# Attention and a two-layer MoE block on one core: the first two chunks interleaved, weights decoded by pairs of steps, and the first batch's GpSimd work moved to VectorE

## The chip, the cores and the metric

The kernel runs on one core of a Trainium2 chip. The time is the device time of one execution, in microseconds; the median over the runs is compared. The core has five engines: TensorE (PE, matmuls), VectorE (DVE), ScalarE (ACT), GpSimd (POOL), and SyncE (SP), which here issues every DMA.

## The reference, cut to what matters

```python
# q, k, v: (8 batches, 8 heads, 576 positions, 64)
q_d = q.reshape(B, H, 144, 4, D).mean(axis=3)          # k_d, v_d likewise
out_d = sm_attn(q_d, k_d, v_d)                         # softmax attention on 144 positions
out_up = np.repeat(out_d, 4, axis=2)
scores = np.where(abs(pos[:, None] - pos[None, :]) < 4, scale * q @ k.T, -1e9)
out_local = softmax(scores) @ v                        # seven keys per position
x = (out_up + out_local).transpose(0, 2, 1, 3).reshape(4608, 512)
h = x @ w_in                                           # 512 x 2048
g = np.maximum(h, 0.0) + alpha * np.minimum(h, 0.0)    # alpha: one number per hidden column
out = g @ w_out                                        # 2048 x 512
```

All inputs are fp32. Both MoE products are made from a high and a low part of each operand: high by high, high by low, low by high, so three matmuls each.

## The kernel before, in words

**Tokens and chunks.** The 4608 tokens are worked on in 18 chunks of 256. A chunk has 8 steps, one for each pair of 128-column blocks of the hidden layer. `h_step` makes 24 matmuls of 128x256 (line L642) into one PSUM tile. After it, ACT multiplies by the slope (L651), DVE takes the maximum (L654, the "relu" below: a tile `t` and two instructions for each step), ACT rounds to the high part `gh` (L656) and POOL subtracts to get the low part `gl` (L97, called through `sub`). `out_step` makes 12 matmuls of 128x512 (L690) into two PSUM tiles that add up over the chunk's 8 steps; after the eighth, ACT copies them to `sg` (L695) and SP stores them (L698). h runs AH = 2 steps ahead of out. The steps are numbered through, so `t8` is the relu of the first step of the second chunk and `t16` that of the third.

**Where x comes from.** The first 576 tokens (batch 0) are made by `first_batch`, four pairs of heads hp 0 to 3, on tiles that lie over the whole batch; this gives x for the first two chunks and a rest of 64 tokens for the third (`place_rest`). All other tokens come in units of 192 tokens, u = 3 to 23, from `local`: products of q and k on DVE (L551, with sums L553), a softmax whose small tiles lie in PSUM bank "l" (`lb`, L566 to L575), products of p and v (L593, L596, L598), a last sum into `x` (L600), then transposes on PE (`xp`), the sum with the downsampled part (`xf`, L615), and high and low parts `xh` (ACT) and `xl` (POOL, L97). A copy of q lies in PSUM bank "q" (`qp`). Chunk 2 needs units 3 and 4, and the downsampled attention of batch 1.

**Downsampled attention.** For batches 1 to 7 and each pair of heads, `load_sums` brings q, k and v in six loads (L228) through a ring of three `ld` buffers. POOL adds four positions into one (L100); what follows uses PE, ACT and a few small DVE instructions (`dnb` L279, `drs` L285).

**Weights.** w_in and w_out come as fp64 words, and are decoded in 32 pieces of 128x512: ACT makes an absolute value (L152), DVE runs four instructions (L153 to L156), ACT makes the high part, and DVE or POOL the low part (L204 for w_out, L210 for w_in on DVE, L97 on POOL). The raw words go through three slots. Pieces come in quarters n = 0 to 3 of the hidden columns, each quarter serving two steps: first four pieces of w_in, then four of w_out.

**First batch's engines.** Tables of letters give POOL (p) or DVE (v) for each pair of heads: sums of q and k of hp 2 and 3 (`FQ`, L408 and L410), sums of v of all pairs (`FV`, L426 and L430), the multiply by the reciprocal (`FMUL`, L454) and the low parts of x (`FLO`, L485) on POOL. `POOL_LO` gives some of the w_in low parts to POOL.

**Order.** Each engine runs its instructions in one fixed order. A scheduler lays that order out when the program is built, from its own model of times and from priorities (`high_priority` offsets such as PP, DP and HP). On the chip an instruction that waits holds up everything behind it on its engine. SP issues the loads and stores one after the other in the same way.

## Time and profile before

| | us |
|---|---|
| median of three runs (1134.49, 1140.88, 1140.39) | 1140.39 |
| profiled execution, its time | 1138.52 |
| profiled execution, span of the trace | 1136.7 |
| PE busy | 1005.7 |
| DVE busy | 861.4 |
| POOL busy | 526.4 |
| ACT busy | 454.7 |
| first relu of chunk 0 starts | 111.9 |
| copy of chunk 0's sums starts | 199.5 |
| copy of chunk 1's sums starts | 248.1 |
| first relu of chunk 2 starts | 251.0 |
| first relu of chunk 3 starts | 320.4 |

A time in the lower rows is counted from the start of the span. The trace's rows name an engine, a line of the kernel, the operation, and the tiles as output<-inputs. In rows of a timeline the first number is the start and the second the duration, and a bracket gives how long the engine had been idle and which instruction or transfer let it go on.

### The profile page before, as it was taken

The page shows a single profiled execution, that of the slowest core. Times are in us where ns is not written, and L with a number is a line of the kernel's source. Part 1 is how long each engine was busy: PE and PEld are TensorE (multiplying, and loading weights), DVE is VectorE, ACT ScalarE, POOL GpSimd, SP SyncE. Part 2 cuts the span into 40 slices and gives each one's busy share as a digit, 9 for nine tenths or more (in the row PEclk, how much of TensorE's full clock was granted, in tenths as well). Part 3 has the DMA queues.
Part 4 walks back from the last instruction along what each step waited for, and adds up shares of the span by engine and source line. Part 5 has one row for each costly group of instructions (what it writes and reads, how often), then busy time and mean ns, then how long its engine had stood idle before and what let it go on. Part 6 is the DMA issues. An engine that isn't in the chain of part 4 may idle for free.

```text
span 1136.7 us, 17891 instructions
## 1 busy us (share of the span) xinstructions
PE 1005.7 (88%) x6402; PEld 879.8 (77%) x6402; DVE 861.4 (76%) x1467; ACT 454.7 (40%) x1223; POOL 526.4 (46%) x633
## 2 busy tenths in 40 slices
PE   5857797898768999889999999989999989999995
PEld 5646675696657898777888888878888878899994
DVE  7999496597847889678878988779887778895110
ACT  5767344242323443333444334344343425333221
POOL 4787474333434644544555543555537244333221
PEclk9756889798968999899999999999999989999998
DMA  8944612222222222221223222323222212100000
GB/s 181 240 150 145 189 43 86 65 83 76 66 92 77 87 100 87 92 87 65 80 95 109 85 80 89 105 76 101 88 92 82 96 58 78 54 19 19 1 20 19
DMA packets 57503, 98.26 MB, mean 86 GB/s; under 512 B 19910, under 2 KB 25286, under 8 KB 57414
## 3 DMA queue, kind: packets, MB, share of 16 engines
q1 hardware_dynamic: 57414, 97.12, 27.1%
q8 instruction: 50, 0.82, 0.3%
q14 instruction: 39, 0.32, 0.1%
HBM read 87.67 MB, written 9.44 MB: 85 GB/s over the span
## 4 chain that ended last, share of the span: by engine, by line
PE 53%; DMA 20%; DVE 11%; POOL 6%; SPq 4%; issue 3%; ACT 2%; ACTq 0%; POOLq 0%; DVEq 0%
PE o L690 26%; PE h L642 22%; DMA ldk<-in_k 10%; DMA q<-in_q 4%; DMA ldq<-in_q 3%; POOL gl L97 2%; SPq L348 2%; DVE temp L155 1%; SPq L499 1%; POOL ldv L100 1%; DVE temp L153 1%; PE pv L266 1%; DVE temp L156 1%; PE xp L607 1%; DMA raw<-in_moe_w_out 1%
## 5 line engine op out<-in xcount | busy, mean ns | idle before, releaser
L97 POOL TENSOR_TENSOR gl<-t,gh 128x512 fp32r<-128x512 f32 x144 | 187.0, 1301 | 238.5 <-ACT gh L656 221.3
L654 DVE SCALAR_TENSOR_TENSOR t<-h,sign,t 128x256 f32<-128x256 f32 x288 | 125.6, 478 | 165.1 <-ACT t L651 159.3
L690 PE MATMUL o<-woh,gl 128*128 128x512 f32 x576 | 193.7, 414 | 45.1 <-POOL gl L97 45.0
L651 ACT ACTIVATE t<-h,slope 128x256 f32<-128x256 f32 x288 | 120.3, 469 | 244.4 <-PE h L642 159.4
L642 PE MATMUL h<-xh,wih 128*128 128x256 f32 x1152 | 201.1, 291 | 1.0 <-DVE t L654 0.7
L690 PE MATMUL o<-woh,gh 128*128 128x512 f32 x576 | 190.2, 407 | 10.3 <-ACT gh L656 10.3
L642 PE MATMUL h<-xh,wil 128*128 128x256 f32 x1152 | 194.3, 288 | 1.0 <-DVE wil L210 1.0
L690 PE MATMUL o<-wol,gh 128*128 128x512 f32 x576 | 191.2, 409 | 0.0
L642 PE MATMUL h<-xl,wih 128*128 128x256 f32 x1152 | 188.0, 285 | 0.0
L642 PEld LDWEIGHTS h<-xh,wih 128*128 128x128 f32 x1152 | 174.0, 196 | 14.4 <-DVE t L654 2.4
L690 PEld LDWEIGHTS o<-woh,gl 128*128 128x128 f32 x576 | 110.4, 195 | 75.8 <-POOL gl L97 51.7
L642 PEld LDWEIGHTS h<-xh,wil 128*128 128x128 f32 x1152 | 163.1, 194 | 1.9 <-DVE wil L210 1.2
L642 PEld LDWEIGHTS h<-xl,wih 128*128 128x128 f32 x1152 | 159.9, 192 | 0.3
L656 ACT CAST gh<-t 128x512 fp32r<-128x512 f32 x144 | 89.4, 621 | 148.5 <-PE o L690 78.6
L551 DVE TENSOR_TENSOR qk<-k,qp 128x768 f32<-128x768 f32 (+1 forms) x126 | 135.0, 1081 | 0.0
L553 DVE TENSOR_REDUCE ls<-qk 128x12 f32<-128x768 f32 (+1 forms) x126 | 133.5, 1080 | 0.2
L690 PEld LDWEIGHTS o<-wol,gh 128*128 128x128 f32 x576 | 111.1, 195 | 24.9 <-issue 0.2
L690 PEld LDWEIGHTS o<-woh,gh 128*128 128x128 f32 x576 | 102.3, 194 | 25.2 <-ACT gh L656 10.5
L598 DVE TENSOR_TENSOR lb<-lb,pv 128x384 f32<-128x384 f32 x210 | 117.9, 562 | 4.0
L100 POOL TENSOR_TENSOR ldk<-ldk 72x256 f32<-72x256 f32 x56 | 45.2, 808 | 153.7 <-DMA ldk<-in_k 143.3
L596 DVE TENSOR_TENSOR pv<-v,lb 128x1152 f32<-128x1152 f32 x84 | 96.8, 1152 | 2.5
L100 POOL TENSOR_TENSOR ldq<-ldq 72x256 f32<-72x256 f32 x56 | 42.8, 774 | 80.6 <-DMA ldq<-in_q 80.4
(146 smaller groups left out, 1194.3 us busy)
## 6 DMA issues: line engine op xcount, KB each, us to landing
k<-in_k SPq DMA_DIRECT2D x41, 384.0 KB
v<-in_v SPq DMA_DIRECT2D x41, 384.0 KB
raw<-in_moe_w_in SPq DMA_DIRECT2D x16, 512.0 KB
raw<-in_moe_w_out SPq DMA_DIRECT2D x16, 512.0 KB
ldq<-in_q SPq DMA_DIRECT2D x56, 144.0 KB
ldk<-in_k SPq DMA_DIRECT2D x56, 144.0 KB
ldv<-in_v SPq DMA_DIRECT2D x56, 144.0 KB
q<-in_q SPq DMA_DIRECT2D x42, 192.0 KB
```

The costliest lines, as they stand in the source:

```text
L97: nc.gpsimd.tensor_tensor(o, a, b, op=ALU.subtract)
L100: nc.gpsimd.tensor_tensor(o, a, b, op=ALU.add)
L348: nc.sync.dma_start(qk[hp][:, i, :, e, :], bass.AP(src.tensor, (2 * hp + e) * HEAD, [[512, 72], [64, 8], [1, 64]]))
L551: nc.vector.tensor_tensor(pr[:, :nd], window(kt, half, d0, nd), qp.unsqueeze(1).to_broadcast([128, nd, 2, 192]), op=ALU.mult)
L553: nc.vector.tensor_reduce(out=s[:, half, d0:d0 + nd, :].rearrange("p a b -> p (a b)"), in_=pr[:, :nd].rearrange("p a h (t d) -> p (a h t) ...
L596: nc.vector.tensor_tensor(pr[:, :nd], window4(vt, half, d0, nd), prob(half, d0, nd), op=ALU.mult)
L598: nc.vector.tensor_tensor(acc, acc, pr[:, i], op=ALU.add)
L642: nc.tensor.matmul(ph[:, j], w[:, m, 128 * o:128 * o + 128], x[:, m, :], start=(i == 0), stop=(i == 11))
L651: nc.scalar.activation(t[:, j], ph[:, j], AF.Copy, scale=slope[:, f:f + 1])
L654: nc.vector.scalar_tensor_tensor(t[:, j], ph[:, j], sign[:, f:f + 1], t[:, j], op0=ALU.mult, op1=ALU.max)
L656: nc.scalar.copy(gh, t)
L690: nc.tensor.matmul(po, g[:, j, 128 * m:128 * m + 128], wo[w][n][:, o, :], start=(f == 0 and i == 0), stop=(f == NF - 1 and i == 2))
```

## The change

**Order of the steps.** `PAIRED = 2` replaces `SEQ`: steps go 0, 8, 1, 9, ..., 7, 15 and then 16, 17, ... Each step pair of the first two chunks uses the same weights. Chunk 0 keeps its two sums in the usual tiles; chunk 1's lie in banks "q" and "l", claimed at the start by a memset of one column. So no unit can use these two banks before chunk 1 is copied out. Unit 3 reads q from SBUF (`UB = {3: 'sx'}`, the 's'), while its softmax still takes bank "l". `place_rest` comes eight positions later.

**Weights.** `load_raw` and `make` replace `load_weights`. A piece of w_in is now 256 columns by 256 rows, and two pieces of w_in and two of w_out make up one step's weights. All low parts are made on DVE. The first loads are ordered by `ORDER`, the rest alternate between w_in and w_out of a step, and the last four pairs come as w_in, w_in, w_out, w_out.

**First batch.** The tables are gone: sums, multiplies and low parts run on DVE for all four pairs. Pair 3's exponential is one instruction on ACT instead of nine. The v tiles have three buffers instead of two.

**A hold.** The first three `ld` tiles of batch 1 are written in one element by DVE from a tile of w_out that belongs to step 5 (`held`, `HOLD = 5`), so that their loads wait for it.

```diff
-FQ = 'vvpp'
-FV = 'pppp'
-FMUL = 'pppp'
-FLO = 'pppp'
-FEXP = 'vvva'
-SEQ = '00001111'
-UB = {}
-GATE = (-1, -1, 2, 3)
+UB = {3: 'sx'}
-DP = (1, 100, 1, 1)
-PP = (1, 1, 250, 250)
-POOL_LO = (1, 5, 1, 1)
-ORDER = 'a0 w w a1 w w a2 b0 w w a3 b1 w w b2 b3'
+PP = (1, 1, 1, 1)
+ORDER = 'a0 i0 a1 b0 o0 a2 b1 a3 b2 i1 b3 o1 i2'
+PAIRED = 2
+HOLD = 5
...
+    def make(which, fp):
...
+            if which == 0:
+                t = t.rearrange("p (k a) -> p k a", k=2)
+                wh, wl = (w[i][n][:, 2 * c:2 * c + 2, 256 * half:256 * half + 256] for i in range(2))
+                decode(t, hi, lo)
+                nc.scalar.copy(wh, f32(t))
+                nc.vector.tensor_tensor(wl, f32(t), f32(wh), op=ALU.subtract)
...
                 ld = one.tile([72, 2, 4, 64], F32, tag="ld", name=f"ld{x}{b}_{hp}{h2}", bufs=LDB)
+                if held:
+                    nc.vector.tensor_copy(ld[:, 0, 0, 0:1], held.pop())
                 nc.sync.dma_start(ld.rearrange("p g f d -> p (g f d)"),
...
-            vt[hp] = st.tile([72, 2, 8, 64], F32, tag="vt", name=f"fv{hp}", bufs=2)
+            vt[hp] = st.tile([72, 2, 8, 64], F32, tag="vt", name=f"fv{hp}", bufs=3)
...
-                        ENG[FQ[hp]].tensor_tensor(s4, lv[:, :, 0:256], lv[:, :, 256:512], op=ALU.add)
+                        nc.vector.tensor_tensor(s4, lv[:, :, 0:256], lv[:, :, 256:512], op=ALU.add)
...
-            ENG[FMUL[hp]].tensor_tensor(p, p, rs.unsqueeze(2).to_broadcast([128, NWIN, KEYS]), op=ALU.mult)
+            nc.vector.tensor_tensor(p, p, rs.unsqueeze(2).to_broadcast([128, NWIN, KEYS]), op=ALU.mult)
...
-                    ENG[FLO[hp]].tensor_tensor(lo, xs, f32(hi), op=ALU.subtract)
+                    nc.vector.tensor_tensor(lo, xs, f32(hi), op=ALU.subtract)
...
     def new_outs(c):
-        if c == 1 and SEQ != "00001111":
+        if 0 < c < PAIRED:
             outs[c] = outs.get(c) or [bank(kind, f"o1_{kind}") for kind in "ql"]
...
+    held.extend(f32(wo[1][HOLD // 2][0:72, 2 * (HOLD % 2) + 1, c:c + 1]) for c in range(LDB))
...
+    order = [NP * c + fp for fp in range(NP) for c in range(PAIRED)] + list(range(PAIRED * NP, NS))
...
+    for c in range(PAIRED):
+        new_outs(c)
+        for po in outs[c]:
             nc.vector.memset(po[:, 0:1], 0.0)
...
-        if i == NP - AH:
+        if i == PAIRED * NP - AH:
             place_rest()
```

The order of the instructions on three engines shows what the diff alone doesn't.

On SP, the loads of batch 1's last pair of heads (`ldq1_30` to `ldv1_31`) and around them, before. In a name, the number after ldq, ldk or ldv is the batch, then come the pair of heads and the half; `v3`, `v4`, `q4` and `k4` are the loads of units 3 and 4, and `in_q`, `in_k`, `in_v` the inputs:

```order
L228 DMA ldq1_30_1525<-in_q 72x512
L228 DMA ldq1_31_1529<-in_q 72x512
L228 DMA ldk1_30_1535<-in_k 72x512
L228 DMA ldk1_31_1539<-in_k 72x512
L228 DMA ldv1_30_1544<-in_v 72x512
L228 DMA ldv1_31_1548<-in_v 72x512
L228 DMA ldq2_00_1757<-in_q 72x512
L228 DMA ldq2_01_1761<-in_q 72x512
L228 DMA ldk2_00_1778<-in_k 72x512
L520 DMA v3_1202<-in_v 128x1x768 x2
L520 DMA v4_1205<-in_v 128x1x768 x2
L499 DMA q4_1342<-in_q 128x1x384 x2
```

And on SP in the changed kernel, the same loads:

```order
L230 DMA ldk1_20_1394<-in_k 72x512
L511 DMA v3_1197<-in_v 128x1x768 x2
L230 DMA ldk1_21_1398<-in_k 72x512
L230 DMA ldv1_20_1403<-in_v 72x512
L230 DMA ldv1_21_1407<-in_v 72x512
L490 DMA q4_1334<-in_q 128x1x384
L511 DMA v4_1200<-in_v 128x1x768 x2
L490 DMA q4_1334<-in_q 128x1x384
L511 DMA k4_1337<-in_k 128x1x768 x2
L230 DMA ldq1_30_1517<-in_q 72x512
L230 DMA ldq1_31_1521<-in_q 72x512
L230 DMA ldk1_30_1527<-in_k 72x512
```

Before, the last pair of batch 1 stood ahead of the loads of units 3 and 4; now it stands behind them. `v3` waits there for the last decoded piece, whose raw words lie in the same buffer, and `q4` and `k4` wait for the last of unit 3's scores on DVE.

On DVE, unit 3's last scores and its softmax, before; `lb3` is the softmax's tile in bank "l", `t9` and `t10` are relus of chunk 1:

```order
L553 TENSOR_REDUCE ls3_1208<-qk3_15_1322 128x12
L654 SCALAR_TENSOR_TENSOR t9_2038<-h9_2013,sign_78,t9_2038 128x256 x2
L561 TENSOR_TENSOR ls3_1208<-ls3_1208,mask_l_1017 128x84
L285 RECIPROCAL drs1_3_1613<-dsm1_3_1612 96x3
L566 TENSOR_REDUCE lb3_1349<-ls3_1208 128x12
L567 TENSOR_TENSOR ls3_1208<-ls3_1208,lb3_1349 128x84
L654 SCALAR_TENSOR_TENSOR t10_2113<-h10_2088,sign_78,t10_2113 128x256 x2
L570 TENSOR_REDUCE lb3_1349<-lex3_1350 128x12
```

And on DVE in the changed kernel; `t7` and `t15` are the last relus of chunks 0 and 1:

```order
L552 TENSOR_TENSOR ls3_1203<-ls3_1203,mask_l_1002 128x84
L643 SCALAR_TENSOR_TENSOR t14_2311<-h14_2286,sign_78,t14_2311 128x256 x2
L287 RECIPROCAL drs1_1_1327<-dsm1_1_1326 96x3
L643 SCALAR_TENSOR_TENSOR t7_2389<-h7_2364,sign_78,t7_2389 128x256 x2
L643 SCALAR_TENSOR_TENSOR t15_2466<-h15_2441,sign_78,t15_2466 128x256 x2
L281 TENSOR_REDUCE dnb1_2_1428<-s1_2_1424 96x3
L287 RECIPROCAL drs1_2_1430<-dsm1_2_1429 96x3
L557 TENSOR_REDUCE lb3_1341<-ls3_1203 128x12
L558 TENSOR_TENSOR ls3_1203<-ls3_1203,lb3_1341 128x84
L561 TENSOR_REDUCE lb3_1341<-lex3_1342 128x12
```

Before, the softmax stood among the relus of chunk 1; now it stands behind the last of them, and 48 rows, from the first one of `lb3` on, lie ahead of the first relu of chunk 2, `t16`: unit 3's softmax and values, unit 4's scores, its softmax and the start of its values. Before, 16 rows lay between `t15` and `t16`.

On POOL, the sums of batch 1's last pair of heads and the low part of the last step of chunk 0 (`gl7`), before:

```order
L100 TENSOR_TENSOR ldv1_30_1544<-ldv1_30_1544 72x2x128
L100 TENSOR_TENSOR s2k1_3_1534<-ldk1_31_1539 72x2x64
L100 TENSOR_TENSOR ldv1_31_1548<-ldv1_31_1548 72x2x128
L100 TENSOR_TENSOR s2v1_3_1543<-ldv1_30_1544 72x2x64
L97 TENSOR_TENSOR gl5_1736<-t5_1734,gh5_1735 128x512
L100 TENSOR_TENSOR s2v1_3_1543<-ldv1_31_1548 72x2x64
L100 TENSOR_TENSOR ldq2_00_1757<-ldq2_00_1757 72x2x128
L100 TENSOR_TENSOR ldq2_01_1761<-ldq2_01_1761 72x2x128
L100 TENSOR_TENSOR ldk2_00_1778<-ldk2_00_1778 72x2x128
L97 TENSOR_TENSOR gl6_1813<-t6_1811,gh6_1812 128x512
L97 TENSOR_TENSOR xl2_1698<-rest_89,xh2_1697 128x4x64
L97 TENSOR_TENSOR gl7_1884<-t7_1882,gh7_1883 128x512
```

And on POOL in the changed kernel; `gl14`, `gl7` and `gl15` are the low parts of the last three steps of the first two chunks:

```order
L87 TENSOR_TENSOR gl14_2313<-t14_2311,gh14_2312 128x512
L87 TENSOR_TENSOR xl2_1690<-rest_89,xh2_1689 128x4x64
L90 TENSOR_TENSOR ldq1_30_1517<-ldq1_30_1517 72x2x128
L90 TENSOR_TENSOR ldq1_31_1521<-ldq1_31_1521 72x2x128
L90 TENSOR_TENSOR ldk1_30_1527<-ldk1_30_1527 72x2x128
L87 TENSOR_TENSOR gl7_2391<-t7_2389,gh7_2390 128x512
L90 TENSOR_TENSOR s2q1_3_1516<-ldq1_30_1517 72x2x64
L90 TENSOR_TENSOR s2q1_3_1516<-ldq1_31_1521 72x2x64
L90 TENSOR_TENSOR s2k1_3_1526<-ldk1_30_1527 72x2x64
L90 TENSOR_TENSOR ldk1_31_1531<-ldk1_31_1531 72x2x128
```

Before, the sums of that pair of heads stood ahead of `gl7` too, but their loads were issued ahead of those of units 3 and 4. Now `gl7`, and behind it `gl15` (five rows below the last one shown), wait for loads that are issued behind `q4`, `v4` and `k4`. Lower down on POOL, the second part of `xl2`, without which chunk 2's x isn't complete, stood ahead of the sums of `ldk2_11`; now it stands behind those of `ldk2_11`, `ldv2_10` and `ldv2_11`. From the first relu of chunk 3 on (the relu of step 24) the rows on DVE are the same in both kernels, and the other engines' rows come together near there too.

More of the change, by code (lines that the diff above doesn't have):

```diff
@@ new lines, in tile_attention_moe, with load_raw @@
+    raws, turns = {}, [0, 0]
+    weights_temp = []
+    def load_raw(which, fp):
+        n = fp // 2
+        if which == 1 and n == 3:
+            pool, tag, bufs = pools[0], ("prod", "vt")[fp % 2], 2
+            raw = [pool.tile([128, 1, 512, 2], I32, tag=tag, name=f"raw1_{fp}{c}", bufs=bufs) for c in range(2)]
+        elif which == 1:
+            t = one.tile([128, 2, 512, 2], I32, tag=f"slot{turns[0] % 3}", name=f"raw1_{fp}")
+            raw = [t[:, c:c + 1] for c in range(2)]
+        else:
+            slot = turns[0] % 3 if n < 3 else 2 + fp % 2
+            t = one.tile([128, 2, 2, 256, 2], I32, tag=f"slot{slot}", name=f"raw0_{fp}")
+            raw = [t[:, c] for c in range(2)]
+        turns[0] += 1
+        src = (w_in, w_out)[which].bitcast(I32)
+        for c in range(2):
+            if which == 0:
+                nc.sync.dma_start(raw[c].rearrange("p k a b -> p k (a b)"),
+                                  bass.AP(src.tensor, 256 * c * 2 * DF + 512 * fp, [[2 * DF, 128], [256 * DF, 2], [1, 512]]))
+            else:
+                row = 256 * fp + 128 * c
+                nc.sync.dma_start(raw[c].rearrange("p k a b -> p (k a b)"), src[row:row + 128, :])
+        raws[which, fp] = raw
@@ L435, in pair @@
             sm = one.tile([128, NWIN], F32, tag="lsm", name=f"fsm{hp}")
-            gate[hp] = sm[:, 0:1]
             rs = one.tile([128, NWIN], F32, tag="lrs", name=f"frs{hp}")
@@ L702, in tile_attention_moe @@
     pools = []
-    gate = {}
-    wl = load_weights()
     load_alpha()
@@ L707, in tile_attention_moe @@
     nc.gpsimd.memset(qd32, 0.0)
+    late_raws = []
     with tc.tile_pool(name="start", bufs=1) as start:
         load_pair, load_windows, pair = first_batch(start)
+        todo = [(w, fp) for fp in range(NP) for w in range(2)]
         for step in ORDER.split():
-            if step == "w":
-                next(wl)
+            kind, i = step[0], int(step[1])
+            if kind in "io":
+                load_raw("io".index(kind), i)
+                todo.remove(("io".index(kind), i))
             else:
-                (load_pair if step[0] == "a" else load_windows)(int(step[1]))
+                (load_pair if kind == "a" else load_windows)(i)
         for hp in range(4):
@@ L718, in tile_attention_moe @@
                     pass
-        while next(wl) != "late":
-            pass
+        for fp in range(NP - 2):
+            for which in range(2):
+                if (which, fp) not in raws:
+                    load_raw(which, fp)
+                make(which, fp)
     build_masks()
@@ L723, in tile_attention_moe @@
     pools.append(late)
-    for _ in wl:
-        pass
+    for which in range(2):
+        for fp in (NP - 2, NP - 1):
+            load_raw(which, fp)
+    for which in range(2):
+        for fp in (NP - 2, NP - 1):
+            make(which, fp)
+    held.extend(f32(wo[1][HOLD // 2][0:72, 2 * (HOLD % 2) + 1, c:c + 1]) for c in range(LDB))
     def place_rest():
```

133 lines of the change are left out of this document (42 added, 91 removed).

## The prediction

> **What bounds the kernel now.** I read first the busy time of each engine by stretches. The columns are the stretch, its length, the busy time of PE, PE's weight loads, DVE, ACT and POOL (with instructions), then PE's granted clock, the DMA share and GB/s:
>
> ```profile
> 0.00:112.00 112.00, 75.16 (x484) 63.20 (x484) 102.13 (x182) 71.78 (x196) 76.55 (x81) 0.72 0.69 175
> 112.00:200.00 88.00, 69.14 (x406) 58.28 (x407) 61.83 (x90) 38.20 (x101) 46.99 (x53) 0.85 0.35 112
> 200.00:252.00 52.00, 46.34 (x271) 40.36 (x271) 38.93 (x69) 15.84 (x43) 15.94 (x18) 0.90 0.23 78
> 252.00:320.00 68.00, 56.12 (x340) 48.64 (x339) 54.38 (x88) 21.61 (x57) 30.09 (x40) 0.90 0.21 69
> 320.00:1137.00 817.00, 758.89 (x4908) 669.31 (x4907) 604.17 (x1042) 307.31 (x830) 356.83 (x443) 0.97 0.22 73
> ```
>
> To 112 us DVE is busy 102.13 of 112 us, so it sets the start. From 112 to 320 no engine is full: PE is idle 36.4 us of 208. From 320 on PE is busy 93% at a clock of 0.97, and only a shift of the start can move that stage. The waits of PE from 100 to 360 us (us in total, times, longest) name what is late:
>
> ```profile
> PE o L690 <- POOL gl L97: 19.3, 4, 5.7
> PE pT L293 <- ACT dp L287: 18.9, 4, 9.3
> PE o L690 <- ACT gh L656: 10.3, 1, 10.3
> ```
>
> So out steps wait for the low part of a relu, and PE's fixed order waits for the downsampled attention. The marks I use are the first relus of chunks 0, 2 and 3 on DVE, and the copies of chunk 0's and 1's sums on ACT:
>
> ```profile
> 111.91 0.47 DVE L654 SCALAR_TENSOR_TENSOR t<-h,sign,t 128x256 f32<-128x256 f32 x1
> ...
> 251.03 0.88 DVE L654 SCALAR_TENSOR_TENSOR t<-h,sign,t 128x256 f32<-128x256 f32 x2 [0.80 <-ACT t L651]
> ...
> 320.43 0.86 DVE L654 SCALAR_TENSOR_TENSOR t<-h,sign,t 128x256 f32<-128x256 f32 x2
> ```
>
> ```profile
> 199.47 0.58 ACT L695 COPY sg<-o 128x512 f32<-128x512 f32 x1
> ...
> 248.08 0.58 ACT L695 COPY sg<-o 128x512 f32<-128x512 f32 x1
> ```
>
> From chunk 3's first relu DVE's rows are the same in both kernels, so the remaining 816.3 us (1136.7 less 320.4) stay, and the whole question is when that relu comes. I follow four legs to it.
>
> **Leg 1, to the first relu.** DVE's instructions there are slower than they can be. By group to 112 us (count | busy, mean ns), with the same forms where nothing stretched them, and one that was stretched:
>
> ```profile
> L155 DVE SCALAR_TENSOR_TENSOR temp<-raw,temp 128x512 int32<-128x512 int32 x23 | 18.7, 813 | 0.1
> L156 DVE SCALAR_TENSOR_TENSOR temp<-raw,temp 128x512 int32<-128x512 int32 x22 | 17.6, 807 | 0.1
> L154 DVE TENSOR_SCALAR temp<-temp 128x512 int32<-128x512 int32 x23 | 17.3, 751 | 0.2
> L153 DVE TENSOR_SCALAR temp<-temp 128x512 f32<-128x512 f32 x24 | 14.1, 591 | 3.2 <-ACT temp L152 3.1
> L204 DVE SCALAR_TENSOR_TENSOR wol<-temp,sign,woh 128x512 fp32r<-128x512 f32 x9 | 9.1, 1032 | 0.0
> L210 DVE TENSOR_TENSOR wil<-temp,wih 128x512 fp32r<-128x512 f32 x8 | 8.1, 1014 | 0.0
> L408 DVE TENSOR_TENSOR fqk<-fqk 72x512 f32<-72x512 f32 x4 | 3.8, 945 | 3.0 <-PE f0T L380 2.0 <-PE f1T L380 0.9
> ...
> L451 DVE TENSOR_REDUCE fsm<-fp 128x9 f32<-128x630 f32 x3 | 2.4, 799 | 0.0
> ```
>
> ```profile
> 7.05 0.69 DVE L408 TENSOR_TENSOR fqk<-fqk 72x512 f32<-72x512 f32 x1 [2.02 <-PE f0T L380]
> ...
> 13.40 0.43 DVE L153 TENSOR_SCALAR temp<-temp 128x512 f32<-128x512 f32 x1 [2.94 <-ACT temp L152]
> 13.87 0.43 DVE L154 TENSOR_SCALAR temp<-temp 128x512 int32<-128x512 int32 x1
> 14.33 0.69 DVE L155 SCALAR_TENSOR_TENSOR temp<-raw,temp 128x512 int32<-128x512 int32 x1
> ...
> 22.36 0.68 DVE L210 TENSOR_TENSOR wil<-temp,wih 128x512 fp32r<-128x512 f32 x1
> 22.96 0.41 DVE L410 TENSOR_TENSOR fs2q<-fqk 72x256 f32<-72x256 f32 x1
> ...
> 38.38 0.74 DVE L204 SCALAR_TENSOR_TENSOR wol<-temp,sign,woh 128x512 fp32r<-128x512 f32 x1
> ...
> 59.04 3.52 DVE L154 TENSOR_SCALAR temp<-temp 128x512 int32<-128x512 int32 x1
> ```
>
> The excess is 23 x 0.12 + 22 x 0.12 + 23 x 0.32 + 24 x 0.16 + 9 x 0.29 + 8 x 0.33 + 4 x 0.26, or 23 us. An instruction of 0.43 us that takes 3.52 has no reason in its own form; I take POOL's work (76.55 us in this stretch) as the cause. That POOL work is nearly all the first batch's, and it goes: -23 us.
>
> By order, 18 of the 32 pieces stand ahead of the first relu now, 24 before. Six pieces less are 6 x (0.43 + 0.43 + 0.69 + 0.69) = 13.4 us less; low parts on DVE stay about even (18 now, 9 + 8 before). The work that comes over: sums of q and k of two pairs 4 x 0.69 + 4 x 0.41 = 4.4; sums of v 4 x 0.69 + 4 x 0.41 = 4.4; four multiplies of 128x630 at the 0.80 of the sum over that shape, 3.2; eight low parts of x of 128x256 at 0.41, 3.3; pair 3's softmax 1.2 more; one low part 0.7. That is 17.2 us, so 3.8 more than the six pieces. DVE's idle 9.9 us may grow, since a faster DVE asks for the same words earlier (the DMA share is 0.69 there already): I add 1.5, with 0 to 7 as bounds. First relu at 111.9 - 23 + 3.8 + 1.5 = 94 us, bounds 89 to 100.
>
> **Leg 2, to the end of both chunks.** PE runs a step in two pieces; the chain of waits shows them:
>
> ```profile
> 222.49 2.80 PE h L642 x24
> 225.29 2.81 PE o L690 x12
> ```
>
> Sixteen steps are 16 x 5.61 = 90 us, so by PE alone both chunks end at about 185 to 187, 61 us ahead of the 248.1 of before. DVE has 14 more pieces (about 3 us each with the low part, 42 us), 16 relus at 0.88 and unit 3's scores in that time, near 90 us as well, so it doesn't delay much. But the low parts do, by POOL's order and the loads. The rows: the pace of six batch-1 loads between the first and the last issue, DMA over ten undisturbed microseconds, and a POOL wait behind v3, v4 and q4:
>
> ```profile
> 138.65 8.57 SPq L228 DMA_DIRECT2D ldq<-in_q  x2
> ...
> 158.32 2.31 SPq L228 DMA_DIRECT2D ldq<-in_q  x2
> ```
>
> ```profile
> 174.00:184.00 10.00, 9.60 (x62) 7.74 (x61) 10.00 (x15) 5.06 (x13) 5.43 (x5) 1.00 0.26 100
> ```
>
> ```profile
> 195.60 0.72 POOL L100 TENSOR_TENSOR ldk<-ldk 72x256 f32<-72x256 f32 x1 [13.88 <-DMA ldk<-in_k]
> ```
>
> Six loads take 19.7 us, 3.3 each. With the hold, and behind the last weights, I put the first batch-1 load at 122 to 125 and its landing at 135; eighteen loads at 3.3 reach 194 at the latest. `gl7` and `gl15` need loads of the last pair, which stand behind v3 (gated by the last decoded piece), q4, v4 and k4 (gated by unit 3's last scores). Both gates are DVE rows some 67 us of clean work behind the first relu, so about 165. The four are 0.79 + 0.39 + 0.79 + 0.79 MB, at 100 GB/s 27 us: `ldq1_30` lands near 196, `ldk1_30` near 202. Before, fewer bytes in the same place made POOL wait 13.88 us. So `gl7` comes near 202 and `gl15`, behind three more loads, at 207 to 211. Two out steps behind them end both chunks at about 210, bounds 187 (the loads are not what waits) to 225.
>
> **Leg 3, to chunk 2's first relu.** Unit 3's softmax needs bank "l", so it starts behind the copy of chunk 1's sums (two of 0.58, 1.2 us). Behind it DVE has 48 rows ahead of that relu; before, PE had chunk 1's steps to do meanwhile, now it has none. DVE's busy time from 112 to 320 us in rows that touch the softmax's tile (three units) and in those of the scores (four units):
>
> ```profile
> 112.00:320.00 208.00, 42.44 (x75) 0.88 0.27 89
> ```
>
> ```profile
> 112.00:320.00 208.00, 49.99 (x48) 0.88 0.27 89
> ```
>
> Softmax and values 42.44 / 3 = 14.1, unit 4's scores 49.99 / 4 = 12.5, and some 7 us for `xf`, the downsampled rows and the start of unit 4's values: 33.6 us. That stretch leaves PE idle for tens of us. What a long idle costs beyond itself:
>
> ```profile
> 334.73 1.22 PE L690 MATMUL o<-woh,gh 128*128 128x512 f32 x2 [10.32 <-ACT gh L656]
> ```
>
> ```profile
> 334.70:340.10 5.40, 5.38 (x21) 4.97 (x22) 3.39 (x9) 2.13 (x7) 4.45 (x7) 0.50 0.36 99
> ```
>
> After 10.32 us idle the granted clock was 0.50 for 5.4 us, which is 2.7 us lost; I take 1 of it for this relu, as h is the first work. [...] `xl2` stands behind three batch-2 sums now: 1 us, bounds 0 to 13.9 by the wait above. So 210 + 1.2 + 33.6 + 1 + 1 = 247, against 251.0: 38 us of lead at chunk 1's end shrink to 4.
>
> **Leg 4, to chunk 3's first relu.** Before it took 69.4 us (251.03 to 320.43), in which DVE was busy 54.38 of 68. By order the changed kernel has some 4 us more DVE work there, and less of the waiting: 71 us, bounds 66 to 74. So 247 + 71 = 318, 2.4 us ahead. Its time is 1138.52 - 2.4, about 1136. The profiled execution lies 1.9 us under the median of 1140.39 and inside the runs shown, so I make no correction; 1% is 11.4 us, about what a measurement can tell.
>
> **Rivals.**
> *The loads don't wait.* If batch 1's loads run ahead of POOL, chunk 1 ends near 187 and the same 37 us of DVE rows follow: relu at 224, or 27 earlier. DVE is then full from the start, with 4 us more work and unit 3's loads behind it, so some 7 us come back: 1138.5 - 20 = 1118. For it: 13.88 us is the only long wait of that kind here. Against: the order of the queue.
> *Slower: the queue reaches further.* If the gate of q4 and k4 comes at 180 instead of 165 (DVE still stretched, or words late), `ldk1_30` lands at 217 and chunk 1 ends at 225: relu at 262, 11 us late, and 4 us more work: 1138.5 + 13 = 1152. It decides once `gl15` ends past 216.
> *POOL isn't what stretches DVE.* Then leg 1 keeps the 23 us, and adds 5: first relu at 117, the gate at 188, and the end as in the last case or worse, 1155 to 1165. The 3.52 us row beside POOL work speaks against it.
>
> **How the numbers follow.** My forecast, near 1136, has a chance of 0.42 (chunk 1 ends between 201 and 219); an early end, 0.38, near 1118 and at best 1100; the two late cases 0.20 together. The range leaves a tenth on each side: 1104 to 1153.
>
> **What would show it.** First relu at 89 to 100 and L154 near 0.43 us; both chunks copied within some 6 us of each other near 210; POOL idle ahead of the sums of `ldq1_30`; no PE work for 25 us or more ahead of step 16; chunk 3's first relu near 318. A copy ahead of 195 or behind 220 makes the forecast wrong; so does a leg 4 outside 66 to 74.

## The result and the profile after

The changed kernel takes 1152.22 us (median of 5 runs, 1150.30 to 1155.10), the kernel before 1140.39 us. The ratio is 1.0119, with a 95% interval of 1.0071 to 1.0167: it is slower by 1.2%, where about 1136 us, and so no measurable change, was forecast. The profiled execution has a span of 1150.3 us against 1136.7.

The same stretches as before, with the same columns (stretch, length, busy PE, weight loads, DVE, ACT, POOL, granted clock, DMA share, GB/s):

```profile
0.00:112.00 112.00, 93.30 (x609) 79.14 (x610) 95.90 (x216) 68.72 (x170) 13.74 (x30) 0.82 0.68 186
112.00:200.00 88.00, 68.05 (x421) 58.09 (x419) 66.45 (x97) 39.16 (x94) 45.50 (x47) 0.92 0.26 86
200.00:252.00 52.00, 20.78 (x90) 15.19 (x91) 28.84 (x47) 13.66 (x47) 22.04 (x35) 0.60 0.27 94
252.00:320.00 68.00, 55.20 (x330) 47.86 (x329) 55.06 (x96) 21.73 (x59) 28.18 (x36) 0.88 0.21 67
320.00:1150.00 830.00, 767.42 (x4956) 677.77 (x4956) 612.95 (x1052) 310.78 (x837) 359.16 (x448) 0.96 0.22 73
```

To 112 us PE does 18 us more than before, and POOL 63 us less. Between 200 and 252 us PE is busy 20.78 of 52 us, where it had been 46.34. Everything that was won early is lost there. PE's waits from 100 to 360 us (us in total, times, longest) show two of the causes, the low parts again (first row) and unit 3's `x` (third row); the 10 us of the second row lie near chunk 3's first relu:

```profile
PE o L679 <- POOL gl L87: 32.0, 4, 17.5
PE h L631 <- DVE t L643: 14.3, 4, 10.0
PE xp L598 <- DVE x L591: 9.7, 2, 8.6
```

The marks of the prediction, on DVE (first relus of chunks 0, 2 and 3, and the second one of chunk 3) and on ACT (the two copies of chunk 1's sums):

```profile
86.91 0.86 DVE L643 SCALAR_TENSOR_TENSOR t<-h,sign,t 128x256 f32<-128x256 f32 x2
...
261.10 0.88 DVE L643 SCALAR_TENSOR_TENSOR t<-h,sign,t 128x256 f32<-128x256 f32 x2 [3.54 <-ACT t L640]
...
338.98 0.88 DVE L643 SCALAR_TENSOR_TENSOR t<-h,sign,t 128x256 f32<-128x256 f32 x2 [9.89 <-ACT t L640]
340.94 0.88 DVE L643 SCALAR_TENSOR_TENSOR t<-h,sign,t 128x256 f32<-128x256 f32 x2
```

```profile
219.69 0.59 ACT L684 COPY sg<-o_q 128x512 f32<-128x512 f32 x1 [3.45 <-DMA out<-sg]
221.16 0.60 ACT L684 COPY sg<-o_l 128x512 f32<-128x512 f32 x1
```

So the lead over the kernel before is 25 us at the first relu and 28 at the copies (219.7 against 248.1), and it is a lag of 10 at chunk 2's first relu (261.1 against 251.0).

The next table lists the marks of all kernels that follow: median and ratio to the kernel before as measured beside it, then from the traces the first relu, the start of the first copy of chunk 1's sums, chunk 2's first relu, and chunk 3's second relu. That last mark is used because a wait of 10 us lies on one side of chunk 3's first relu in one kernel and on the other side in another. Each mark comes from one execution, and the executions of one kernel differ by 5 to 16 us in time (the kernel before: 1129.39 to 1142.38 within one round), so differences of a few us between marks are not read.

The kernels were measured in six rounds, with the kernel before again in each. Its median was 1140.39 us beside the changed kernel and 1135.14 to 1136.96 us in the other rounds. So a difference to the changed kernel comes out 2 to 4 us larger by the medians than by the ratios; where the two differ, both ends are given. Each kernel of the table also has its own order of instructions, laid out anew by the scheduler. e10 and e23 leave out work that the result needs.

| kernel | median us | ratio (95%) | relu 0 | copy 1 | relu chunk 2 | 2nd relu chunk 3 |
|---|---|---|---|---|---|---|
| before | 1140.39 | 1 | 112 | 248 | 251 | 334 |
| changed | 1152.22 | 1.0119 (1.0071 to 1.0167) | 87 | 220 | 261 | 341 |
| e1 unit 4's loads last | 1151.56 | 1.0143 (1.0095 to 1.0191) | 87 | 225 | 264 | 345 |
| e2 unit 3 off the bank | 1135.40 | 1.0001 (0.9977 to 1.0026) | 87 | 226 | 259 | 326 |
| e3 before, moved work | 1120.30 | 0.9838 (0.9778 to 0.9897) | 104 | 220 | 230 | 311 |
| e4 no hold | 1147.96 | 1.0099 (1.0064 to 1.0135) | 97 | 219 | 259 | 340 |
| e5 not interleaved | 1130.07 | 0.9944 (0.9926 to 0.9963) | 87 | 243 | 242 | 325 |
| e8 e3 and interleaved | 1140.46 | 1.0039 (1.0005 to 1.0073) | 106 | 217 | 257 | 335 |
| e9 e5 without hold | 1133.65 | 0.9966 (0.9932 to 1.0000) | 100 | 228 | 234 | 319 |
| e10 no loads of unit 4 | 1142.93 | 1.0060 (1.0032 to 1.0087) | 89 | 211 | 251 | 331 |
| e12 before, all moved work | 1116.08 | 0.9827 (0.9789 to 0.9865) | 101 | 223 | 228 | 310 |
| e16 units 3 and 4 off the banks | 1136.45 | 0.9999 (0.9976 to 1.0023) | 87 | 228 | 262 | 319 |
| e17 e16 without hold | 1124.15 | 0.9904 (0.9872 to 0.9936) | 96 | 225 | 243 | 320 |
| e19 e17 not interleaved | 1125.01 | 0.9879 (0.9829 to 0.9929) | 97 | 241 | 244 | 320 |
| e20 e12 and units off the banks | 1116.23 | 0.9833 (0.9790 to 0.9876) | 102 | 228 | 230 | 313 |
| e23 no batch-1 sums on POOL | 1121.84 | 0.9887 (0.9844 to 0.9930) | 88 | 205 | 246 | 321 |

### The profile page after: what moved, and what is told of

The parts are those of the page before. It is cut to its first block, busy times and chain, and to the rows that moved or that the text cites. A ratio compares the mean times of both kernels' runs of the same rounds, so it can differ in the third digit from the quotient of the medians.

```text
span 1150.3 us, 17872 instructions
## 1 busy us (share of the span) xinstructions
PE 1004.7 (87%) x6402; PEld 878.1 (76%) x6402; DVE 859.2 (75%) x1506; ACT 454.1 (39%) x1204; POOL 468.6 (41%) x596
## 4 chain that ended last, share of the span: by engine, by line
PE 50%; DMA 21%; DVE 11%; POOL 7%; issue 4%; SPq 4%; ACT 2%; ACTq 0%; POOLq 0%; DVEq 0%
PE o L679 23%; PE h L631 21%; DMA ldk<-in_k 10%; DMA ldq<-in_q 4%; POOL gl L87 2%; DMA q<-in_q 2%; DMA raw<-in_moe_w_out 2%; DVE qk L542 1%; DMA ldv<-in_v 1%; PE pv L268 1%; POOL ldv L90 1%; PE xp L598 1%; DVE t L643 1%; DVE lb L589 1%; DVE temp L148 1%
## 5 line engine op out<-in xcount | busy, mean ns | idle before, releaser
L87 POOL TENSOR_TENSOR gl<-t,gh 128x512 fp32r<-128x512 f32 x144 | 190.4, 1325 | 335.8 <-ACT gh L645 311.5
L679 PE MATMUL o<-woh,gl 128*128 128x512 f32 x544 | 182.1, 413 | 60.2 <-POOL gl L87 60.0
L679 PE MATMUL o<-woh,gh 128*128 128x512 f32 x544 | 178.9, 406 | 0.0
L679 PE MATMUL o<-wol,gh 128*128 128x512 f32 x544 | 178.7, 406 | 0.0
L679 PEld LDWEIGHTS o<-woh,gl 128*128 128x128 f32 x544 | 103.8, 195 | 90.0 <-POOL gl L87 67.2
L542 DVE TENSOR_TENSOR qk<-k,qp 128x768 f32<-128x768 f32 (+1 forms) x120 | 127.9, 1077 | 0.0
L679 PEld LDWEIGHTS o<-wol,gh 128*128 128x128 f32 x544 | 104.3, 193 | 23.5
L679 PEld LDWEIGHTS o<-woh,gh 128*128 128x128 f32 x544 | 95.6, 192 | 13.6 <-issue 0.8
L90 POOL TENSOR_TENSOR ldk<-ldk 72x256 f32<-72x256 f32 x56 | 42.2, 753 | 145.1 <-DMA ldk<-in_k 136.4
L587 DVE TENSOR_TENSOR pv<-v,lb 128x1152 f32<-128x1152 f32 x84 | 96.8, 1152 | 2.5
```

What stands on the lines that cost most here:

```text
L87: nc.gpsimd.tensor_tensor(o, a, b, op=ALU.subtract)
L90: nc.gpsimd.tensor_tensor(o, a, b, op=ALU.add)
L542: nc.vector.tensor_tensor(pr[:, :nd], window(kt, half, d0, nd), qp.unsqueeze(1).to_broadcast([128, nd, 2, 192]), op=ALU.mult)
L587: nc.vector.tensor_tensor(pr[:, :nd], window4(vt, half, d0, nd), prob(half, d0, nd), op=ALU.mult)
L679: nc.tensor.matmul(po, g[:, j, 128 * m:128 * m + 128], wo[w][n][:, o, :], start=(f == 0 and i == 0), stop=(f == NF - 1 and i == 2))
```

## The experiments

### The moved work alone (e3, e12)

```diff
 # before
-FQ, FV, FMUL, FLO = 'vvpp', 'pppp', 'pppp', 'pppp'
+FQ, FV, FMUL, FLO = 'vvvv', 'vvvv', 'vvvv', 'vvvv'
 # e12 also
-FEXP = 'vvva'
-POOL_LO = (1, 5, 1, 1)
+FEXP = 'vvvv'
+POOL_LO = (0, 0, 0, 0)
```

> The kernel before, with nothing changed but the first batch's GpSimd work (sums, multiplies, low parts of x) put on VectorE. Theory P (GpSimd's work stretches VectorE's instructions): the mean of the L154 instructions up to 112 us falls from 751 ns to under 500, VectorE's total of work to the first relu grows by about 17 us and loses about 23, so the first relu comes at about 106 instead of 111.9 us and the time moves by -8 to +2 us. Rival N (something else stretches them): the mean stays over 650 ns, the first relu comes at about 128 us and the time grows by 12 us or more.

> The kernel before with all of the engine change and none of the order change: sums, multiplies and low parts of x on VectorE, pair 3's exponential as one instruction on ScalarE, and every low part of w_in on VectorE. Against the kernel with only the first three (1120.3 us). If VectorE's 3 us for the five low parts is all there is, 1118 to 1126; if GpSimd's low parts of w_in were still stretching VectorE's instructions, the mean of L154 to 112 us falls from 481 ns to 430 and the time by another 2 to 5 us.

Measured: 0.9838 and 0.9827, or 15 to 18 us (e3) and 20 us (e12) faster than the kernel before. In e3, by group to 112 us:

```profile
L155 DVE SCALAR_TENSOR_TENSOR temp<-raw,temp 128x512 int32<-128x512 int32 x20 | 16.3, 813 | 0.0
...
L153 DVE TENSOR_SCALAR temp<-temp 128x512 f32<-128x512 f32 x22 | 11.1, 502 | 6.3 <-ACT temp L152 6.2
L154 DVE TENSOR_SCALAR temp<-temp 128x512 int32<-128x512 int32 x20 | 9.5, 481 | 0.0
L210 DVE TENSOR_TENSOR wil<-temp,wih 128x512 fp32r<-128x512 f32 x7 | 6.6, 946 | 0.1
```

L154 went from 751 to 481 ns, though DVE took on the other engine's work. So the first batch's work on POOL was what stretched this row, and the third rival of the prediction (that it isn't) falls. But not every row is free: L155 stays at 813 ns, and L210 only falls from 1014 to 946, where such rows take 675 and 676 ns in the changed kernel (shown below). Batch 1's attention has begun by then in e3 (its first `dnb` row is at 91.50 us, against 103.84 before), so its sums on POOL run beside this decode; in the changed kernel, where the hold keeps them back, POOL is busy 5.58 us up to the first relu. That these sums are what is left of the stretch in e3 wasn't tested.

The first relu came 8 us earlier, near the 6 expected. The time fell by more than the 8 us that the expectation allows at most, as chunk 0 (188 instead of 199 us) and chunk 2 (230 instead of 251) gain as well. e12's further gain over e3 is within both intervals; L154 came to 464 ns instead of the 430 named, with L155 at 785 and L210 at 890.

So the part of the change that moves work is a gain of some 1.7%, and the rest of the change costs 33 to 36 us (by the ratios 1.0119 and 0.9827, or 1152.2 less 1116.1).

### The interleaving (e5, e8, e9)

```diff
 # after: e5, and e9 without the hold
-PAIRED = 2
+PAIRED = 1
 # e3: e8
-SEQ = '00001111'
-UB = {}
+SEQ = '01010101'
+UB = {3: 'sx'}
```

> The changed kernel with chunks 0 and 1 one after the other again (PAIRED = 1): the paired decode, the VectorE work and the hold stay, no bank is claimed. Theory B (the claimed banks put units 3 and 4 behind chunk 1): the first relu stays at 87 us, unit 3's softmax stands among chunk 1's relus, chunk 2's first relu follows the copy of chunk 1's sums by under 15 us (40 in the changed kernel), and the time falls by 30 us or so, to about 1120. Rival D (interleaving is what lets the decode keep up, so that taking it away starves chunk 0): chunk 0 takes 100 us or more from its first relu, chunk 1's copy stays near 220, and the time stays over 1135.

> The kernel before with the first batch's GpSimd work on VectorE and with chunks 0 and 1 interleaved two steps at a time in the claimed banks; unit 3's q is read from SBUF, and the decode by quarters and the free loads stay as before. Against the same kernel without the interleaving (1120.3 us). Theory B: chunk 2's first relu comes some 40 us behind the copy of chunk 1's sums, and the time is 20 to 30 us longer, 1140 to 1150. If the interleaving itself is harmless and the hold or the paired decode costs the time, it stays within 6 us of 1120.

> The changed kernel with chunks 0 and 1 one after the other and without the hold. If the hold only delays batch 1's attention, this is 4 to 10 us faster than the same kernel with the hold. If it protects the weights, the first relu comes later than 92 us (97 in the interleaved kernel without the hold) and the time is the same or longer.

Interleaving costs 20 to 23 us on top of e3 (1140.46 against 1120.30), as expected, and taking it away from the changed kernel gains 20 to 22 (1130.07). What e5 shows is not what either theory said. Rival D was right that chunk 0 starves: it takes 105 us from its first relu to its copy (87 to 192). Chunk 1 is copied 24 us later than in the changed kernel. Yet chunk 2 begins 19 us earlier, ahead of that copy. The first relu of chunk 2, and then the copy, in e5:

```profile
242.05 0.87 DVE L643 SCALAR_TENSOR_TENSOR t<-h,sign,t 128x256 f32<-128x256 f32 x2
```

```profile
243.43 0.59 ACT L684 COPY sg<-o 128x512 f32<-128x512 f32 x1 [0.50 <-PE o L679]
```

So when chunks 0 and 1 end says little about the time. What counts is when units 3 and 4 and batch 1's attention are ready for chunk 2. In the six kernels with interleaving in the claimed banks (changed, e1, e4, e8, e10, e23), chunk 2's first relu comes 39 to 41 us behind the first copy, wherever that copy lies (205 to 225 us). Without interleaving the distance is between -1 and 10.

The hold is not the cause: without it the interleaved kernel is 2 to 4 us faster (e4, 1147.96) and the other 2 to 4 us slower (e9), which the intervals don't tell from nothing. Of e9's two expectations the gain of 4 to 10 us failed, and the other (first relu later than 92, time the same or longer) was met. e4's failed, except for the first relu: the time didn't fall by 10 to 20 us, and the copy of chunk 1's sums came at 219 and not by 205. It waits for a store there:

```profile
218.63 0.59 ACT L684 COPY sg<-o_q 128x512 f32<-128x512 f32 x1 [7.23 <-DMA out<-sg]
```

What e4 did show is what the hold is worth early: its first relu comes at 97 instead of 87.

> The changed kernel without the hold on batch 1's first three loads. By its order, batch 1's loads then all stand ahead of v3, q4, v4 and k4 on SP, and the low parts of the last steps no longer stand behind batch 1's sums on GpSimd. Theory Q: GpSimd starts on batch 1 before 100 us, the copy of chunk 1's sums comes by 205 us, and the time falls by 10 to 20 us, to about 1136. What the hold could be worth: if the early loads take the transfers' time from the weights, the first relu comes 5 us or more later than 87 us and L147 and L148 are stretched by GpSimd's sums; a time of 1150 or more would mean that this eats the whole gain.

```diff
-    held.extend(...)
```

### The loads (e1, e10)

```diff
 # e1: in local, u = 3: loads of unit 4 placed behind "place"; and in load_q and load_kv
+        if u == 4:
+            nc.gpsimd.tensor_copy(qt[0:72, :, 0, 0:1], last[0][:, :, 0:1])   # last: the v sum of batch 1, pair 3
 # e10: in local, instead of the loads of unit 4
+        if u == 3:
+            tiles[4, "q"], tiles[4, "k"], tiles[4, "v"] = qt, kt, vt
```

> The changed kernel, with the loads of unit 4 (v4, q4, k4) made to wait for batch 1's last sum on GpSimd, so that SP issues batch 1's last six loads ahead of them. Theory Q (the queue: gl7 and gl15 wait on GpSimd behind sums whose loads stand behind q4, v4 and k4): GpSimd's idle time of 17.2 us ahead of the sums of ldq1_30 falls to under 6, the copy of chunk 1's sums comes at about 202 instead of 220.9 us, chunk 2's first relu at about 244 instead of 261, and the time falls by some 15 us to about 1137. Rival R (the end of both chunks is set by VectorE's rows and the loads only hide behind them): the copy stays within 5 us of 220 and the time within 5 us of 1152. Rival S (unit 4's loads are then the late ones): chunk 1 ends at 202 but chunk 2's first relu stays near 258.

> The changed kernel without the loads of unit 4, which is computed from unit 3's q, k and v instead (left out: 2 MB of transfers; unit 4's x is that of unit 3). It takes the transfers away instead of moving them ahead of the stores. Theory Q: gl7 and gl15 no longer wait, the store of chunk 0 isn't blocked either, both chunks are copied by about 204 us, chunk 2's first relu follows at about 244, and the time falls by some 15 us to 1137. If the copies come by 204 and the time still stays over 1147, the gain is given back behind chunk 2, and the end of the first two chunks isn't what the time hangs on.

The changed kernel has the queue as the prediction described it. SP's issues of v3, of the first half of q4, of k4 and of the next `ldq` and `ldk`:

```profile
171.14 1.18 SPq L511 DMA_DIRECT2D v<-in_v  x2
...
174.20 0.56 SPq L490 DMA_DIRECT2D q<-in_q  x1
...
182.54 7.47 SPq L511 DMA_DIRECT2D k<-in_k  x2
190.11 2.70 SPq L230 DMA_DIRECT2D ldq<-in_q  x2
192.90 16.80 SPq L230 DMA_DIRECT2D ldk<-in_k  x2
```

And the waits they cause on POOL and PE; `gl7`, whose `gh7` was rounded by 184.1 us, ran on POOL at 207.71, behind the sums that had waited:

```profile
205.66 1.40 POOL L90 TENSOR_TENSOR ldq<-ldq 72x256 f32<-72x256 f32 x2 [17.21 <-DMA ldq<-in_q]
```

```profile
209.02 1.22 PE L679 MATMUL o<-woh,gl 128*128 128x512 f32 x2 [17.48 <-POOL gl L87]
```

e1 moved the loads of unit 4 behind batch 1's, and POOL's wait went; PE finished chunk 1's last products at about 203 us, 15 earlier. Nothing came of it. The loads of unit 4 now stand ahead of the stores of chunk 0, and ACT's copy of chunk 1 needs one of their two buffers:

```profile
204.68 5.65 SPq L519 DMA_DIRECT2D k<-in_k  x2
210.43 2.33 SPq L699 DMA_DIRECT2D out<-sg  x1
```

```profile
224.96 0.59 ACT L696 COPY sg<-o_q 128x512 f32<-128x512 f32 x1 [14.05 <-DMA out<-sg]
```

The wait went from one end of the queue to the other. By its numbers (copy within 5 us of 220, time within 5 of 1152) e1 is what rival R expected, but what the copy waits for is the store, and not VectorE's rows. In e10, which has no such loads at all (unit 4 is computed from unit 3's inputs), most of both waits is gone: PE's longest one for a low part there is 4.07 us, and the copy waits for the store as in the changed kernel (3.45 us there):

```profile
210.79 0.58 ACT L686 COPY sg<-o_q 128x512 f32<-128x512 f32 x1 [3.48 <-DMA out<-sg]
```

The copy is 9 us earlier than in the changed kernel, chunk 2's first relu 10 us and the time 7 to 9 us. Theory Q holds with a smaller size than expected (211 and 1143 instead of 204 and 1137). In e10 too, `v3` is issued only at 174 us, the sums of `ldq1_30` start at 196 instead of 205.7, and POOL waits for a load of the same pair until 203.

### The claimed banks (e2, e16, e17, e19)

```diff
 # e2: unit 3's softmax and sums in SBUF
-        lb = unit_bank("l", u, f"lb{u}")
+        lb = late.tile([128, 120], F32, ...) if u == 3 else unit_bank("l", u, f"lb{u}")
+            if u == 3:
+                acc = x[:, 3 * half:3 * half + 3].rearrange("p t h d -> p h t d")
 # e16: e2, and unit 4's q read from SBUF;  e17: e16 without the hold;  e19: e17 with PAIRED = 1
-UB = {3: 'sx'}
+UB = {3: 'sx', 4: 'sx'}
```

> The changed kernel, with unit 3's softmax and its accumulator in SBUF instead of PSUM bank l, so that unit 3 need not wait for the copy of chunk 1's sums. Theory B (behind chunk 1's end some 40 us of VectorE rows stand in series, because the bank was claimed): unit 3's x is finished before the copy of chunk 1's sums, the copy itself stays near 220, chunk 2's first relu comes at about 247 instead of 261, and the time falls by some 12 us to about 1140. If the bank is not what holds chunk 2 up, the first relu stays within 4 us of 261 and the time near 1152.

> The changed kernel with unit 3's softmax in SBUF, and unit 4's q read from SBUF too, so that neither unit 3 nor unit 4's scores touch the banks of chunk 1; only unit 4's softmax still does. Theory B: with unit 3's softmax alone moved, chunk 2's first relu still came 32 us behind the copy of chunk 1's sums, because unit 4's scores needed bank q; now the scores run in VectorE's idle time ahead of the copy, the distance falls to 12 to 16 us, the first relu comes at about 241 us, and the time falls to about 1122, below both kernels. If the order of VectorE's rows, and not the banks, sets the distance, it stays over 27 us and the time near 1135.

> As the kernel with units 3 and 4 off the banks, without the hold. SP then issues batch 1's loads ahead of unit 4's, so the copy of chunk 1's sums no longer waits for gl7 and gl15, but for the stores behind unit 4's loads, near 219 as before without the hold; chunk 2's first relu 10 to 16 us behind it at about 232, and the time 3 to 8 us below the same kernel with the hold. If the early loads stretch the decode as before (first relu at 97 instead of 87), and VectorE is the bound, the two are equal within 3 us.

> The kernel with units 3 and 4 off the banks and without the hold, but with chunks 0 and 1 one after the other. Measured so far without the hold: not interleaved with units in the banks 1133.65 us, interleaved in the banks 1147.96, interleaved with units 3 and 4 off the banks 1124.15. Theory B (the interleaving itself gains, and the claimed banks cost more than it gains): without the interleaving, taking the units off the banks changes little, and the time stays within 5 us of 1133. If reading from SBUF is what gained the 24 us, this kernel comes to 1125 or below.

In the changed kernel DVE stands idle for 22 us ahead of the end of chunk 1, and starts on unit 3's softmax only when the copy frees the bank:

```profile
211.71 0.60 DVE L281 TENSOR_REDUCE dnb<-s 96x3 f32<-96x432 f32 x1 [22.01 <-PE s L262]
...
221.79 0.31 DVE L557 TENSOR_REDUCE lb<-ls 128x12 f32<-128x84 f32 x1 [6.62 <-ACT sg L684]
```

Taking unit 3 off the bank (e2) gains 13 to 17 us, to 1135.40, near the 12 expected. But chunk 2's first relu moves by 2 us only instead of 14; the gain shows at chunk 3's second relu (326 against 341). That more of unit 4's and 5's work is done by then is my reading, and wasn't traced. e16 missed its expectation (241 and 1122): no bank holds unit 3 or unit 4's scores, DVE runs them in the gap, and the first relu stays at 262. Two rows of ACT and one of PE show what is late there:

```profile
228.02 0.59 ACT L687 COPY sg<-o_q 128x512 f32<-128x512 f32 x1 [12.49 <-DMA out<-sg]
228.50 0.69 ACT L298 COPY th<-pT 72x288 f32<-72x288 f32 x2
```

```profile
228.95 0.75 PE L268 MATMUL pv<-th,s2v 72*64 72x144 f32 x4 [8.03 <-ACT th L298]
```

The copy of chunk 1's sums waits on ACT for a store, and the downsampled attention of batch 1, which chunk 2 needs, stands behind it on ACT. So there are two chains to chunk 2, units 3 and 4 through the banks and batch 1 through its late loads, and each hides the other: with only the loads early (e4) chunk 2's first relu comes at 259, with only the banks free (e16) at 262. With both shortened (e17) it comes at 243 and the time is 1124.15, 24 to 28 us less than the changed kernel and 22 to 24 less than e4, which differs only in the banks. In size e17's expectation was missed too: copy at 219, first relu at 232, and 3 to 8 us less than e16, against 225, 243 and 12.

e19 shows that this isn't a gain of interleaving: without it the same kernel takes 1125.01, and the intervals overlap. Its expectation (within 5 us of e9's 1133.65) failed: units off the banks gain 9 to 10 us without interleaving as well, and the time named for the rival, 1125, is what came. So part of e17's gain is not the freeing of claimed banks; whether the reading from SBUF gives it, or that the two units no longer share the banks with each other, wasn't separated. Interleaving in free banks is worth nothing that was measured here, and in the claimed ones it costs 14 us (e4 against e9) to 22 (changed against e5).

### The decode behind the first relu, and the best parts together (e23, e20)

```diff
 # e23: in load_sums, batch 1 only
-                add(lv[:, :, 0:128], lv[:, :, 0:128], lv[:, :, 128:256])
-                add(s2[:, :, 64 * h2:64 * h2 + 64], ld[:, :, 0, :], ld[:, :, 1, :])
+                nc.scalar.copy(s2[:, :, 64 * h2:64 * h2 + 64], ld[:, :, 0, :])
 # e20: e12 with units 3 and 4 off the banks as in e16
```

> The changed kernel without batch 1's sums on GpSimd (left out: of each four positions only one is kept, copied by ScalarE). Between 95 and 175 us of the changed kernel the rest of the decode ran on VectorE beside those sums, at 723 ns for L146, 897 for L148 and 1225 for the low parts of w_in, against 0.43, 0.69 and 0.68 us undisturbed. Theory P2 (these sums are what stretched it, as the first batch's work did in the kernel before): the means fall to under 480, 750 and 800 ns, the last decoded piece and unit 3's last scores are done some 12 us or more earlier, and the load of q4 is issued by 163 us instead of 174. Rival W (the words' arrival sets the pace of the decode): the means fall but q4 is issued later than 170 us.

> The kernel before with all of the moved work on VectorE (1116.08 us alone) and with units 3 and 4 off the banks, not interleaved: the parts that gained, together. In the kernel with the paired decode and no hold, taking the units off the banks gave 8.6 us without interleaving. If that adds up, about 1108; if unit 3 is already free of the banks' waits here (chunk 2's first relu came 4.8 us behind the copy of chunk 1's sums), it stays within 4 us of 1116.

In the changed kernel DVE's decode up to the first relu (0 to 87 us) has none of the stretch that the kernel before showed:

```profile
L147 DVE SCALAR_TENSOR_TENSOR temp<-raw,temp 128x512 int32<-128x512 int32 x17 | 11.3, 675 | 0.0
L148 DVE SCALAR_TENSOR_TENSOR temp<-raw,temp 128x512 int32<-128x512 int32 x16 | 10.8, 677 | 0.0
L145 DVE TENSOR_SCALAR temp<-temp 128x512 f32<-128x512 f32 x18 | 7.5, 419 | 2.4 <-ACT temp L144 2.4
L146 DVE TENSOR_SCALAR temp<-temp 128x512 int32<-128x512 int32 x17 | 7.0, 414 | 0.0
...
L204 DVE TENSOR_TENSOR wil<-temp,wih 128x512 fp32r<-128x512 f32 x8 | 5.4, 676 | 0.0
```

From 95 to 175 us, beside batch 1's sums and the low parts on POOL, the same rows are slower:

```profile
L148 DVE SCALAR_TENSOR_TENSOR temp<-raw,temp 128x512 int32<-128x512 int32 x14 | 12.6, 897 | 0.0
L147 DVE SCALAR_TENSOR_TENSOR temp<-raw,temp 128x512 int32<-128x512 int32 x14 | 11.1, 791 | 0.1
L146 DVE TENSOR_SCALAR temp<-temp 128x512 int32<-128x512 int32 x13 | 9.4, 723 | 0.1
...
L145 DVE TENSOR_SCALAR temp<-temp 128x512 f32<-128x512 f32 x12 | 8.5, 711 | 6.3 <-ACT temp L144 6.3
L204 DVE TENSOR_TENSOR wil<-temp,wih 128x512 fp32r<-128x512 f32 x7 | 8.5, 1225 | 0.0
L212 DVE SCALAR_TENSOR_TENSOR wol<-temp,sign,woh 128x512 fp32r<-128x512 f32 x7 | 7.2, 1036 | 0.1
```

Those six groups hold 57.3 us, where 14 pieces at the clean means are 41 to 42. In e23, without the sums, they hold 49.4: L145 falls to 418 ns, L148 to 695, L204 to 843 and L146 to 584, but L147 and L212 rise to 892 and 1156. Of the three means that theory P2 named, one (L148) fell below its bound. So the sums were about half of the stretch and not all of it; what is left beside DVE there are POOL's low parts of the relus, which take 2098 ns each in e23 (1558 in the changed kernel in the same window) against 1286 in the long later stage. The load of v3, gated by the last decoded piece, is issued at 162 instead of 171 us:

```profile
162.10 1.17 SPq L515 DMA_DIRECT2D v<-in_v  x2
```

Unit 3's last product, which gates q4, ends at 168.2 instead of 174.2, so 6 us earlier and not 12. q4 is issued at 175, as rival W had it, but for another reason: SP's order in e23 puts it behind loads that wait for a buffer. The time, 1121.84, is no measure of the stretch alone, since the low parts no longer wait behind sums on POOL either (the copy comes at 205).

e20 is as fast as e12 (1116.23 against 1116.08): the two gains don't add up, and chunk 2's first relu comes at 230 as against 228, so the banks weren't what held it there. e12 and e20 are the fastest kernels here, 1.7% under the kernel before.

## Why the prediction was wrong

**The sum.** The profiled execution takes 1152.09 us where 1136 was forecast. Of these 16 us, leg 1 gives -7, leg 2 +17, leg 3 +4, leg 4 +7, and the rest of the kernel -5.

**Leg 1 was right in its cause and too careful in its size.** The first relu came at 86.9 us (forecast 94, bounds 89 to 100), L146 near 0.41 us. Some 5 of the 7 us are in the count: the trace has 14 low parts of weights ahead of that relu instead of 18, and 16 to 18 of each decoding row instead of 18.

**Leg 2 failed, and in one term: the 14 pieces behind the first relu "at about 3 us each, 42 us".** From 95 to 175 us they took 57.3 us of DVE. I had taken POOL's work in leg 1 as what stretches DVE (e3 bore that out, 751 to 481 ns for L154), took it off the account because the first batch's work was gone, and didn't see that the hold puts batch 1's sums beside just these pieces. So the gates, "some 67 us of clean work" behind the first relu, came up to 87 us behind it, of which DVE was busy 80. Unit 3's last product ended at 174.2 instead of 165, although the first relu was 7 us early. q4's first half was issued then, and k4 at 182.5, behind v4 in the queue. Everything behind the gate kept its distance: the sums of `ldq1_30` started at 205.7 instead of 196, `gl15` came at 215 instead of 207 to 211, and the copy of chunk 1's sums at 219.7 instead of 210. So the queue (27 us of loads at 100 GB/s, `gl7` and `gl15` behind the sums) was right: POOL waited 17.21 us and PE 17.48. e23 takes away the sums and half of the stretch, e10 the loads, and both move the copy: to 205 and 211. What the other half of the stretch is wasn't shown, with POOL's low parts as the candidate. Nor does the hold alone bring the sums there: in e4, without it, L148 still takes 813 ns and L204 1134 from 97 to 175 us.

**Leg 3 was right in its mechanism and 4 us short, 41 us against 37.** DVE's 48 rows (55 instructions) took 35.8 us, 32.3 of them busy (33.6 worked out); the softmax began 2.1 us behind the start of the copy instead of 1.2. The relu then waited 3.54 us for its h, where I had put 2 us for the clock and `xl2` together: PE had waited 2.76 us for `xl` (the row stands in the last section), and all of that h ran at a granted clock of 0.50.

**Leg 4 was put against a mark that didn't hold.** From chunk 2's first relu to chunk 3's first it took 77.9 us instead of 71, outside the 66 to 74 that the prediction allowed. But the wait of 10 us that stood behind that relu in the kernel before (and which I had quoted) stands ahead of it now. To chunk 3's second relu it took 79.8 us against 83.2 before, so the stage itself was 3 us shorter.

**The rest was not constant.** From chunk 3's second relu to the end the kernel before takes 802.5 us and the changed one 809.4. In all kernels of the table that stretch lies between 800 and 817 us. "The remaining 816.3 us stay" was good to some 8 us either way, with nearly the same rows on DVE; why this varies wasn't tried. As each trace is one execution, and those of one kernel differ by as much, the kernels need not be the cause.

The second rival, the queue that reaches further, is what happened in kind, with the reason given there ("DVE still stretched") and the sign (`gl15` ends at 216.1, just past 216). Its chance was a share of 0.20, which was too low. That its numbers fit to 1 us (chunk 2's first relu at 261, worked out 262; the time 1152, worked out 1152) is in part luck. The gate came at 174, not at 180, and chunk 1 ended at 220, not at 225; leg 3 was 4 us longer than the rival had it, and leg 4 and the rest differed from it as told above. Its own terms, 11 us late and 4 us more work, add up to 15 and not to the 13 that it uses.

The 28 us of lead at the copies are lost in the 39 to 41 us that all kernels with units 3 and 4 in the claimed banks have behind them; the kernel before has 3.

What stays open: e9 and e12 differ in the decode by pairs of steps, the loads' order, some priorities and unit 3's q in SBUF, and e12 is 16 to 18 us faster; which of these costs that wasn't separated.

## What to carry to other kernels

Before two stages are packed together to end early, ask what the next stage needs, and what of it ran in the slack that goes: here units 3 and 4 and batch 1's attention had been hidden behind chunk 1, and the claimed banks and the late loads moved them behind it. If an engine was slow because another one worked beside it, price its later work by what works beside it then, not by the clean rows (here 57.3 us against 41 to 42). A kernel with one queue for loads and stores and short rings need not lose a wait when loads are put in another order (in e1 and e4 a wait for a store, of 14.05 and 7.23 us, took its place); look for the store, and the engine that waits for the store, and what stands behind that.
